# Attention in fewer, longer runs under the first dense layer, and lower halves of weights on VectorE during their conversion

## The chip, the cores and the metric

One core of one Trainium2 chip. The time is in device microseconds (us), the median of three runs: 896.46 before the change (895.49 to 898.31). All shares, spans and rows come from one profiled execution.

## The reference

Three stages follow each other. Sparse attention over 4 batches, 8 heads, 576 positions, 64 wide; half of the heads see the last 32 positions, the other half every 32nd. Its output, as 2304 tokens of 512, goes through a dense layer and then through a mixture of eight experts with a greedy assignment of tokens.

```python
scores = scale * np.matmul(q, k.transpose(0, 1, 3, 2))
attn = softmax(np.where(masks, scores, -1e9))          # local or strided mask by head
x = (attn @ v).transpose(0, 2, 1, 3).reshape(2304, 512)
h = x @ w_in                                           # 512 x 2048, float64 inputs
x = np.maximum(0.01 * h, h) @ w_out                    # 2048 x 512, float64 inputs
order = np.argsort(-(x @ w_gate).flatten())            # greedy: 8 experts, 288 tokens each
out[mask] = np.maximum(x[mask] @ w1[e], 0.0) @ w2[e]   # for each expert e
```

## The kernel before

**Attention** works on 16 units (a batch and two heads, one unit per 128 columns of the model width), each in two groups of two or three tiles. `attention()` is a pipeline of steps, one group entering per step: `a_tr` transposes queries and keys (L123), `a_qk` makes the scores of each tile for two heads (L167) and then masks, reduces (VectorE, L158) and exponentiates them (ScalarE, L160), `a_norm` divides on GpSimd (L182), `a_pt` transposes the probabilities (L195, with fillers L193 in the first five units), `a_pv` makes the value products (L210) and writes the tokens' upper and lower halves (L234, L235). In the program a float32 product of L167 or L210 is one instruction; the profile counts two for each.

**The dense layer** works in six blocks of 384 tokens and 16 slices n of 128 hidden columns each. Each 32-bit product is made of three: upper with upper, upper with lower, lower with upper half. `g1(n)` is 4 x 3 products into one PSUM bank (L374 to L376), the activation (L382 to L385) and then `g2(n)` adds 3 x 3 products to three banks of 512 columns, tag p2, kept for a whole block (L398 to L400, copied out at L405 and L407). Slice n = 16 begins block 1, and needs 16 finished attention groups (DONE); blocks 3 to 5 need 32.

**The weights** come as float64. `conversion()` makes 32 float32 tiles of 128 x 512 (a WI and a WO for each n of block 0): a load of 512 KB issued on GpSimd's queue into one of two buffers (L307, L310), ScalarE (L321), three VectorE instructions (L323 to L325), which free the buffer for the load after the next. `split()` then makes a tile's upper half on ScalarE (L350; or VectorE, L352) and its lower half on GpSimd (L353). CONV counts conversions.

**What sets the order.** Generators are advanced from the loop at the end: per piece of the dense layer a credit is added, and each whole credit advances attention by one piece, a `yield` of `attention()`. The first loop runs attention until DONE is 8. From this text a scheduler fixes each engine's own order of instructions: it takes in time what has its inputs and its buffer ready. PSUM buffers are shared by tag: units 0 to 4 take scores of their second group and the second transposed probabilities from the three banks of tag p2, which the dense layer's blocks use too.

From n = 48 on (second half of the dense layer and the experts) the text is the same before and after.

Of the kernel before, what the change touches and what calls it, by code (L numbers as in the profile page):

```python
# [7 lines left out]
F32 = mybir.dt.float32  # L8
# [18 lines left out]
def body(ctx, tc, q, k, v, w_in, w_out, w_gate, w1, w2, out):  # L27
    nc = tc.nc
# [51 lines left out]
    def xtile(j):  # L80
        if j not in XH:
            if j in (2, 3):
                XH[j], XL[j] = (xa.tile([128, 4, BLK], F32R, name="x" + x, tag=f"x{x}{j}") for x in "hl")
            else:
                XH[j], XL[j] = (xp.tile([128, 4, BLK], F32R, name="x" + x, tag="x" + x) for x in "hl")
        return XH[j], XL[j]
# [51 lines left out]
    def group(u, g):  # L138

        if u % 4 < 2:  # L140
            return 96, 128, [(96 * i, 96 * i, ml0 if i == 0 else ml, i) for i in range(3 * g, 3 * g + 3)]
        w = 18 * RG[2 * g][1]
        return w, w, [(18 * RG[i][0], 32 + 18 * RG[i][0], msf, i) for i in ((0, 1), (2, 3, 4))[g]]
# [3 lines left out]
    def a_qk(u, g):  # L147
        nq, nk, tl = group(u, g)
        n = len(tl)
        tag = "p2" if u < 5 and g else "pS"  # L150
        p = [ps.tile([128, 4, 128], F32, name=f"pS{h}", tag=tag, bufs=BUFS[tag]) for h in range(2)]
        s = at.tile([126, 2, 3, 128], F32, name="sc", tag="sc", bufs=3)
        mx = at.tile([126, 3, 2, 3], F32, name="mx", tag="mx", bufs=4)
        SC[u, g] = s, mx

        def score(i, m):
            for h in range(2):
                nc.vector.tensor_tensor_reduce(s[:nq, h, i, :nk], p[h][:nq, i, :nk], m[:nq, :nk], -0.125,  # L158
                                               3.0e38, OP.add, OP.min, mx[:nq, 0, h, i:i + 1])
                nc.scalar.activation(s[:nq, h, i, :nk], s[:nq, h, i, :nk], AF.Exp,  # L160
                                     bias=mx[:nq, 0, h, i:i + 1], scale=-1.0,
                                     accum_out=mx[:nq, 1, h, i:i + 1])

        for i, (q0, k0, m, _) in enumerate(tl):
            for h in range(2):
                r = slice(64 * h, 64 * h + 64)
                nc.tensor.matmul(p[h][:nq, i, :nk], QK[u][r, 0, 32 + q0:32 + q0 + nq],  # L167
                                 QK[u][r, 1, k0:k0 + nk], start=True, stop=True)
            if u < 2 and i:
                nc.tensor.matmul(p[0][:, 3], ident, QK[u][:, 0, 32:160], start=True, stop=True)  # L170
            yield
        for i, t in enumerate(tl):
            score(i, t[2])

# [26 lines left out]
    def a_pv(u, g):  # L201
        b, c = divmod(u, 4)
        nq, nk, tl = group(u, g)
        n = len(tl)
        t = PT.pop((u, g))
        tag = "p1" if u < 2 else "pT"
        p = ps.tile([128, 3 * 126], F32, name="pX", tag=tag, bufs=BUFS[tag])
        for i, tt in enumerate(tl):
            for h in range(2):
                nc.tensor.matmul(p[64 * h:64 * h + 64, i * nq:i * nq + nq], VT[u][:nk, tt[3], h, :],  # L210
                                 t[:nk, h, i, :nq], start=True, stop=True)
            if i == 0:
                yield
        pieces = []
        if c < 2:
            s0 = b * S + 288 * g
            o = 0
            while o < 288:
                j, a0 = divmod(s0 + o, BLK)
                w = min(288 - o, BLK - a0)  # L220
                pieces.append((p[:, o:o + w], *(x[:, c, a0:a0 + w] for x in xtile(j))))
                o += w
        else:
            r0, nr = 14 * g, n * nq // 18
            i0 = 0
            while i0 < 18:
                j, a0 = divmod(b * S + 32 * i0, BLK)
                i1 = min(18, i0 + (BLK - a0) // 32)
                pieces.append((p[:, :n * nq].rearrange("p (r i) -> p r i", i=18)[:, :, i0:i1],
                               *(x[:, c, a0:a0 + 32 * (i1 - i0)].rearrange("p (i r) -> p r i", r=32)[:, r0:r0 + nr]  # L230
                                 for x in xtile(j))))
                i0 = i1
        for src, dh, dl in pieces:
            (nc.scalar.copy if u else nc.vector.tensor_copy)(dh, src)  # L234
            nc.vector.tensor_sub(dl, src, dh.bitcast(F32))  # L235

    seq = [(u, g) for u in range(16) for g in range(2)]
    DONE = [0]

    def attention():  # L240

        for u in range(2):
            a_load(u)
        for u in range(2):
            v_load(u)
        for t in range(3):
            a_tr(0, t)
            yield
        n = len(seq)
        for s in range(n + 3):  # L250
            cur, mid, old = (seq[x] if 0 <= x < n else None for x in (s, s - 2, s - 3))
            u, g = cur or (99, 0)
            A = a_qk(u, g) if cur else iter(())
            V = a_pv(*old) if old else iter(())
            if u + 1 < 16 and s >= 1:
                a_tr(u + 1, g)
                yield
            if cur:
                next(A)
                yield  # L260
            if mid:
                a_pt(*mid, 0)
                yield
            if cur:
                next(A, None)
                yield
            if old:
                next(V)
                yield
            if u + 1 < 16 and g == 1:  # L270
                a_tr(u + 1, 2)
                yield
            if cur:
                next(A, None)
                yield
            if mid:
                a_pt(*mid, 1)
                yield
            for _ in A:
                pass  # L280
            if s < 1:
                a_tr(u + 1, g)
                yield
            if cur:
                a_norm(u, g)
            for _ in V:
                pass
            if old:
                DONE[0] += 1
            yield  # L290
            if g == 0 and u + 2 < 16:
                a_load(u + 2)
                v_load(u + 2)
# [49 lines left out]
    CONV = [0]  # L343

    def split(pool, src, tag, n):

        hi = pool.tile([128, 512], F32R, name="hi", tag=tag + "h", bufs=2)
        lo = pool.tile([128, 512], F32R, name="lo", tag=tag + "l", bufs=2)
        if n or EARLY[0]:
            nc.scalar.activation(hi, src, AF.Copy)  # L350
        else:
            nc.vector.tensor_copy(hi, src)  # L352
        nc.gpsimd.tensor_sub(lo, src, hi.bitcast(F32))  # L353
        return hi, lo


# [5 lines left out]
    def prep(n):  # L362

        if n < 96:
            SI[n] = split(xp, WI[n % 16], "wi", 0)
# [66 lines left out]
    def logits(pl, gs, f):  # L432

        if f % 4 == 2 and f > 3 or f == 15:
            c = f // 4 - (f < 15)
            for a in range(4):
                nc.tensor.matmul(pl[32 * a:32 * a + 32], V[:, 4 * c + a], gs[c][:, a], start=(c == 0), stop=(c == 3))

# [81 lines left out]
    for a in range(64, 128, 32):  # L520
        nc.vector.tensor_add(sel32, sel32, ident[:, a:a + 32])
    V = consts.tile([128, 16, 32], F32, name="V")
    nc.gpsimd.memset(V, 0.0)

    def gate_out():
        for f in range(0, 16, 3):
            fs = range(f, min(f + 3, 16))
            yield from gate([WO[x] for x in fs], V[:, f:f + len(fs), :8])

    A, Cv = attention(), conversion()  # L530
    bg = []
    for n, _ in enumerate(A):
        if n % 10 == 0:
            next(Cv, None)
        if DONE[0] >= 8:
            break
    credit = 0.0
    for n, _ in enumerate(mlp()):
        st = STEP[0]
        EARLY[0] = st < 20  # L540
        FIRST[0] = st >= 16
        if st < 16:
            if n == 0:
                next(Cv, None)
            credit += 0.9 if DONE[0] < 16 else 0
        elif st < 64:
            credit += 0.5 if DONE[0] < 32 else 0
        if n == 20:
            for a in range(4):
                nc.sync.dma_start(WB[32 * a:32 * a + 32, :, 8 * a:8 * a + 8], w_gate.rearrange("(b j) e -> j b e", j=32))  # L550
        if n == 98:
            bg.append(gate_out())
        if bg and n % 2 == 0:
            if next(bg[0], 1) == 1:
                bg.pop(0)
        while credit >= 1:
            next(A, None)
            credit -= 1
# [507 lines left out]
```

## Time and profile before

| what | value |
|---|---|
| median of three runs | 896.46 us (895.49 to 898.31) |
| the profiled execution's own time | 891.85 us |
| its span, first to last instruction | 890.1 us |
| TensorE busy, mean granted clock | 842.4 us (95%), 0.978 |
| VectorE, ScalarE, GpSimd busy | 544.8, 441.5, 492.1 us |

How to read it: a busy TensorE is not one at its peak, since each product's end is modelled and overlaps the next product's start; the distance from one start to the next tells what a product costs. Idle time of an engine off the critical path costs nothing. The profiled execution is 4.6 us under the median.

### The profile page before, as it was taken

To read this page: it belongs to the slowest core of one execution; us is meant where nothing else is said; L and a number is where in the kernel's file an instruction comes from. 1 tells how busy PE (TensorE), PEld (TensorE's weight loads), DVE (VectorE), ACT (ScalarE), POOL (GpSimd) and SP (SyncE) were. 2 spreads that over 40 slices of the span, in tenths; PEclk is the share of its full clock that TensorE was granted. 3 is DMA by queue.
4 is the path that set the end of the run, shared out by engine and by line. 5 is a ranking of instruction groups with operands and counts; after the bars stand their busy time and mean duration, and the time that the engine had idled before them with its cause. 6 is when DMAs were issued, how large, how long until landed. Compare 5 with 4: busy or idle time off the path is not lost. (4 is left out here: it accounts for less than half of the span.)

```text
span 890.1 us, 17029 instructions
## 1 busy us (share of the span) xinstructions
PE 842.4 (95%) x6272; PEld 710.9 (80%) x6272; DVE 544.8 (61%) x1552; ACT 441.5 (50%) x1098; POOL 492.1 (55%) x402
## 2 busy tenths in 40 slices
PE   8799999899999999999999999997999999999994
PEld 5677766677777787788989777775899999899994
DVE  5787888865546565475645546454758878772320
ACT  5787667464546455444555323332544444444641
POOL 2655646564555565544645355575648547558731
PEclk8999989999999999999999999999899999999998
DMA  8587554420122000044000004362546445546510
GB/s 193 145 199 175 143 137 137 129 63 14 29 46 79 17 6 10 1 160 160 1 1 1 19 1 166 109 205 92 166 147 192 147 133 182 173 146 206 181 52 27
DMA packets 95411, 93.18 MB, mean 105 GB/s; under 512 B 66144, under 2 KB 74336, under 8 KB 95328
## 3 DMA queue, kind: packets, MB, share of 16 engines
q1 hardware_dynamic: 87648, 65.88, 26.0%
q0 software_dynamic: 7680, 26.22, 9.6%
q8 instruction: 49, 0.80, 0.4%
q14 instruction: 34, 0.28, 0.1%
HBM read 76.35 MB, written 15.73 MB: 103 GB/s over the span
## 5 line engine op out<-in xcount | busy, mean ns | idle before, releaser
L353 POOL TENSOR_TENSOR lo<-WI,hi 128x512 fp32r<-128x512 f32 x96 | 127.5, 1328 | 98.9 <-DVE hi L352 58.2
L353 POOL TENSOR_TENSOR lo<-WO,hi 128x512 fp32r<-128x512 f32 x96 | 125.9, 1312 | 88.3 <-ACT hi L350 88.1
L859 POOL TENSOR_TENSOR wlo<-raw,whi 128x1024 fp32r<-128x1024 f32 x48 | 116.8, 2445 | 26.7 <-ACT whi L858 21.7
L350 ACT ACTIVATE hi<-WO 128x512 fp32r<-128x512 f32 x96 | 60.6, 631 | 101.3 <-PE q L961 49.2
L374 PE MATMUL p<-xh,hi 128*128 128x384 f32 x192 | 75.7, 395 | 5.3 <-DVE g L383 5.3
L916 PE MATMUL g<-hh,whi 128*128 128x288 f32 x256 | 78.8, 308 | 0.4 <-DVE exl L879 0.4
L893 PE MATMUL g<-exh,whi 128*128 128x288 f32 x256 | 78.6, 308 | 0.0
L894 PE MATMUL g<-exl,whi 128*128 128x288 f32 x256 | 76.8, 301 | 0.0
L917 PE MATMUL g<-hl,whi 128*128 128x288 f32 x256 | 76.2, 298 | 0.4 <-DVE hl L901 0.4
L895 PE MATMUL g<-exh,wlo 128*128 128x288 f32 x256 | 76.3, 298 | 0.0
L918 PE MATMUL g<-hh,wlo 128*128 128x288 f32 x256 | 75.7, 296 | 0.0
L160 ACT ACTIVATE sc<-sc,mx 96x128 f32<-96x128 f32 (+2 forms) x176 | 67.6, 388 | 15.0 <-DVE mx L158 15.0
L858 ACT ACTIVATE whi<-raw 128x1024 fp32r<-128x1024 f32 x64 | 67.3, 1053 | 2.9 <-DMA raw<-in_moe_w_dram 2.9
L376 PE MATMUL p<-xh,lo 128*128 128x384 f32 x192 | 66.3, 345 | 1.4 <-POOL lo L353 1.2
L421 PE MATMUL p<-xh,hi 128*128 128x384 f32 x192 | 66.4, 346 | 0.0
L375 PE MATMUL p<-xl,hi 128*128 128x384 f32 x192 | 65.8, 343 | 0.2 <-DVE xl L235 0.2
L423 PE MATMUL p<-xh,lo 128*128 128x384 f32 x192 | 64.7, 337 | 0.7 <-POOL lo L353 0.7
L398 PE MATMUL p<-hi,gh 128*128 128x512 f32 x144 | 64.3, 446 | 0.7 <-ACT gh L384 0.7
L422 PE MATMUL p<-xl,hi 128*128 128x384 f32 x192 | 64.4, 335 | 0.0
L182 POOL TENSOR_TENSOR sc<-sc,mx 96x384 f32<-96x384 f32 (+2 forms) x64 | 52.2, 832 | 21.4 <-DVE mx L180 15.2
L932 POOL DMA_INDIRECT out_dram<-o,idx x24 | 24.3, 1011 | 70.4 <-ACT o L908 58.4
L400 PE MATMUL p<-hi,gl 128*128 128x512 f32 x144 | 57.4, 398 | 0.0
(210 smaller groups left out, 2294.3 us busy)
## 6 DMA issues: line engine op xcount, KB each, us to landing
raw<-in_moe_w_dram SPq DMA_DIRECT2D x64, 512.0 KB
wraw<-in_moe_w_in_dram POOLq DMA_DIRECT2D x16, 512.0 KB
wraw<-in_moe_w_out_dram POOLq DMA_DIRECT2D x16, 512.0 KB
g<-g3d SPq DMA_DIRECT2D x16, 384.0 KB
rawq<-in_q_dram SPq DMA_DIRECT2D x32, 144.0 KB
rawk<-in_k_dram SPq DMA_DIRECT2D x32, 144.0 KB
x2d<-x SPq DMA_DIRECT2D x18, 256.0 KB
g3d<-gh SPq DMA_DIRECT2D x16, 192.0 KB
```

The costliest lines, as they stand in the source:

```text
L160: nc.scalar.activation(s[:nq, h, i, :nk], s[:nq, h, i, :nk], AF.Exp, bias=mx[:nq, 0, h, i:i + 1], scale=-1.0, accum_out=mx[:nq, 1, h, i:i ...
L353: nc.gpsimd.tensor_sub(lo, src, hi.bitcast(F32))
L374: nc.tensor.matmul(p1, wh[:, cs], xh[:, c], start=(c == 0), stop=False)
L421: nc.tensor.matmul(p1, wh[:, cs], xh[:, c], start=(c == 0), stop=False)
L858: pin(nc.scalar.activation(hi, raw, AF.Copy))
L859: pin((nc.vector if n in (5, 7) else nc.gpsimd).tensor_sub(lo, raw, hi.bitcast(F32)))
L893: nc.tensor.matmul(p, wh, xh[:, c], start=(c == 0), stop=False)
L894: nc.tensor.matmul(p, wh, xl[:, c], start=False, stop=False)
L895: nc.tensor.matmul(p, wl, xh[:, c], start=False, stop=(c == 3))
L916: nc.tensor.matmul(p, wh, hh[:, j], start=(j == 0), stop=False)
L917: nc.tensor.matmul(p, wh, hl[:, j], start=False, stop=False)
L918: nc.tensor.matmul(p, wl, hh[:, j], start=False, stop=(j == 7))
```

## The change

All scores of a group (two or three tiles, two heads) form one piece, and all its value products one. A step of attention then has five or six pieces in place of eight or nine, and the credits fall from 0.9 to 0.6 and from 0.5 to 0.33; conversions start every six pieces of the first loop, not ten. DONE is counted right behind the value products. Lower halves go to VectorE while CONV is at most 31, which is 31 of the 192 (16 of WI, 15 of WO).

```diff
@@ a_qk
             if u < 2 and i:
                 nc.tensor.matmul(p[0][:, 3], ident, QK[u][:, 0, 32:160], start=True, stop=True)
-            yield
+        yield
         for i, t in enumerate(tl):
             score(i, t[2])
@@ a_pv
                                  t[:nk, h, i, :nq], start=True, stop=True)
-            if i == 0:
-                yield
@@ attention
             if cur:
                 next(A, None)
-                yield
             if old:
-                next(V)
+                a_pv(*old)
+                DONE[0] += 1
                 yield
             if u + 1 < 16 and g == 1:
                 a_tr(u + 1, 2)
                 yield
-            if cur:
-                next(A, None)
-                yield
             if mid:
                 a_pt(*mid, 1)
                 yield
-            for _ in A:
-                pass
...
-            for _ in V:
-                pass
-            if old:
-                DONE[0] += 1
-            yield
@@ split
-        nc.gpsimd.tensor_sub(lo, src, hi.bitcast(F32))
+        (nc.gpsimd if CONV[0] > 31 else nc.vector).tensor_sub(lo, src, hi.bitcast(F32))
@@ the loops at the end
-        if n % 10 == 0:
+        if n % 6 == 0:
             next(Cv, None)
...
-            credit += 0.9 if DONE[0] < 16 else 0
+            credit += 0.6 if DONE[0] < 16 else 0
         elif st < 64:
-            credit += 0.5 if DONE[0] < 32 else 0
+            credit += 0.33 if DONE[0] < 32 else 0
```

In the changed file lines behind `a_pv` are lower: L374 to L376 become L361 to L363, L398 to L400 become L385 to L387, L323 to L325 become L310 to L312, L353 becomes L340, L383 and L385 become L370 and L372.

**The order, place one.** TensorE in block 1, before: scores (pS) of one tile between products of g2.

```order
L398 MATMUL p_2379<-hi,gh 128x512
L399 MATMUL p_2379<-lo,gh 128x512
L400 MATMUL p_2379<-hi,gl 128x512
L167 MATMUL pS_3072<-qk 108x108
L167 MATMUL pS_3073<-qk 108x108
L398 MATMUL p_2380<-hi,gh 128x512
L399 MATMUL p_2380<-lo,gh 128x512
L400 MATMUL p_2380<-hi,gl 128x512
```

The same group's scores with the change, the three tiles in one run:

```order
L385 MATMUL p_2377<-hi,gh 128x512
L386 MATMUL p_2377<-lo,gh 128x512
L387 MATMUL p_2377<-hi,gl 128x512
L167 MATMUL pS_3088<-qk 108x108
L167 MATMUL pS_3089<-qk 108x108
L167 MATMUL pS_3088<-qk 108x108
L167 MATMUL pS_3089<-qk 108x108
L167 MATMUL pS_3088<-qk 108x108
L167 MATMUL pS_3089<-qk 108x108
L385 MATMUL p_2378<-hi,gh 128x512
```

From the slice n = 17 to the end of attention the runs of attention between dense products are 109 before and 76 with the change; in these runs the change has 4 more transposes (L123) and 6 more of probabilities (L195), and as many scores and value products.

**Place two.** TensorE at the start of block 0, before. p_1056, p_1057 and p_1058 are the block's three banks of tag p2; the pP there is the last of units 0 to 4, of tag p2 too.

```order
L400 MATMUL p_1056<-hi,gl 128x512
L193 MATMUL pP<-ident 128x128 x3
L195 MATMUL pP<-ident,sc 128x96 x3
L398 MATMUL p_1057<-hi,gh 128x512
L399 MATMUL p_1057<-lo,gh 128x512
L400 MATMUL p_1057<-hi,gl 128x512
L210 MATMUL pX<-pt,vt 64x96 x3
L374 MATMUL p_1110<-xh,hi 128x384
L398 MATMUL p_1058<-hi,gh 128x512
```

The same pP with the change stands at the end of block 0 (p_1056 is its third bank, p_2234 the first slice of block 1):

```order
L385 MATMUL p_1056<-hi,gh 128x512
L386 MATMUL p_1056<-lo,gh 128x512
L193 MATMUL pP<-ident 128x128 x3
L195 MATMUL pP<-ident,sc 128x96 x3
L387 MATMUL p_1056<-hi,gl 128x512
L210 MATMUL pX<-pt,vt 64x96 x11
L123 MATMUL pT<-ident,rawq 128x96 x2
L123 MATMUL pT<-ident,rawk 128x96 x2
L361 MATMUL p_2234<-xh,hi 128x384
L195 MATMUL pP<-ident,sc 128x96 x3
```

Before, at the first product of slice n = 16, nine products of g2 of block 0 are still to come; with the change they stand ahead of this place. With the change no attention instruction stands on TensorE from the first quarter of the slice n = 4 to this place. Between it and the second slice of block 1 stand 34 scores, 37 value products, 29 transposes of probabilities and 32 transposes of queries and keys, and the last three quarters of the slice n = 16 among them; ScalarE has there 34 exponentials, 12 copies of pt, 12 of xh, 8 of qk and one upper half.

**Place three.** VectorE in the last conversions of block 0, before:

```order
L383 TENSOR_TENSOR g<-p_2086,g 128x384
L325 SCALAR_TENSOR_TENSOR WI<-wraw,cg 128x512
L385 TENSOR_TENSOR gl<-g,gh 128x384
L323 TENSOR_SCALAR cg<-cg 128x512
L324 SCALAR_TENSOR_TENSOR cg<-wraw,cg 128x512
L325 SCALAR_TENSOR_TENSOR WO<-wraw,cg 128x512
L323 TENSOR_SCALAR cg<-cg 128x512
```

And with the change:

```order
L312 SCALAR_TENSOR_TENSOR WI<-wraw,cg 128x512
L310 TENSOR_SCALAR cg<-cg 128x512
L311 SCALAR_TENSOR_TENSOR cg<-wraw,cg 128x512
L340 TENSOR_TENSOR lo<-WI,hi 128x512
L312 SCALAR_TENSOR_TENSOR WO<-wraw,cg 128x512
L340 TENSOR_TENSOR lo<-WO,hi 128x512
L310 TENSOR_SCALAR cg<-cg 128x512
L370 TENSOR_TENSOR g<-p_2126,g 128x384
L311 SCALAR_TENSOR_TENSOR cg<-wraw,cg 128x512
```

Two lower halves per pair of conversions stand among the conversion's own three instructions. GpSimd's order has, in this stretch, only loads and the divisions of attention.

## Rows read from the trace of the kernel before

**Rows 1.** Windows: length; busy PE, PEld, DVE, ACT, POOL; clock; DMA share, GB/s.
```profile
150.00:184.00 34.00, 28.53 (x179) 21.90 (x179) 29.07 (x55) 18.46 (x44) 19.62 (x19) 0.95 0.35 103
184.00:374.00 190.00, 190.00 (x1373) 149.69 (x1372) 103.81 (x341) 99.31 (x299) 104.39 (x93) 1.00 0.12 31
```

**Rows 2.** Timeline, TensorE: value products among dense ones; start, us, instruction, count.
```profile
243.27 0.55 PE L210 MATMUL pX<-pt,vt 128*64 128x96 f32 x8
243.75 0.50 PE L398 MATMUL p<-hi,gh 128*128 128x512 f32 x1
...
337.26 0.39 PE L400 MATMUL p<-hi,gl 128*128 128x512 f32 x1
337.58 0.39 PE L210 MATMUL pX<-pt,vt 128*64 128x96 f32 x4
337.89 0.50 PE L398 MATMUL p<-hi,gh 128*128 128x512 f32 x1
338.23 0.39 PE L399 MATMUL p<-lo,gh 128*128 128x512 f32 x1
338.46 0.39 PE L400 MATMUL p<-hi,gl 128*128 128x512 f32 x1
```

**Rows 3.** Groups of TensorE before 184.2 us; then the timeline behind it.
```profile
L374 PE MATMUL p<-xh,hi 128*128 128x384 f32 x64 | 26.9, 420 | 5.3 <-DVE g L383 5.3
```
```profile
184.32 0.44 PE L374 MATMUL p<-xh,hi 128*128 128x384 f32 x1
```

**Rows 4.** Timeline, VectorE: block 0's first activation; the twelfth conversion's last instruction.
```profile
71.96 0.56 DVE L383 TENSOR_TENSOR g<-p,g 128x384 f32<-128x384 f32 x1
...
80.84 1.48 DVE L325 SCALAR_TENSOR_TENSOR WO<-wraw,cg 128x512 int32<-128x512 int32 x1
```

**Rows 5.** Timeline: a lower half on GpSimd, and VectorE beside it.
```profile
127.35 1.75 POOL L353 TENSOR_TENSOR lo<-WO,hi 128x512 fp32r<-128x512 f32 x1 [1.60 <-ACT hi L350]
```
```profile
127.88 1.50 DVE L323 TENSOR_SCALAR cg<-cg 128x512 int32<-128x512 int32 x1
```

**Rows 6.** Timeline: two loads into one buffer, and conversions on VectorE about them.
```profile
163.06 0.81 POOL L307 DMA_DIRECT2D wraw<-in_moe_w_in_dram  x1 [2.83 <-DVE WI L325]
...
170.61 0.79 POOL L307 DMA_DIRECT2D wraw<-in_moe_w_in_dram  x1 [2.70 <-DVE gl L385]
```
```profile
164.31 1.42 DVE L325 SCALAR_TENSOR_TENSOR WO<-wraw,cg 128x512 int32<-128x512 int32 x1
...
169.36 0.68 DVE L325 SCALAR_TENSOR_TENSOR WI<-wraw,cg 128x512 int32<-128x512 int32 x1
...
177.12 0.65 DVE L325 SCALAR_TENSOR_TENSOR WI<-wraw,cg 128x512 int32<-128x512 int32 x1
```

**Rows 7.** Two lines' VectorE subtractions: least, median, longest ns; starts; shape.
```profile
L859 DVE TENSOR_TENSOR wlo<-raw,whi x16: 1215/1223/3835, 631.3 to 858.4; 128x1024 fp32r<-128x1024 f32 x16
```
```profile
L385 DVE TENSOR_TENSOR gl<-g,gh x48: 508/558/1645, 73.4 to 373.3; 128x384 fp32r<-128x384 f32 x48
```

**Rows 8.** Groups of ScalarE: count, busy us, mean ns, idle before, releaser.
```profile
L160 ACT ACTIVATE sc<-sc,mx 96x128 f32<-96x128 f32 (+2 forms) x176 | 67.6, 388 | 15.0 <-DVE mx L158 15.0
...
L350 ACT ACTIVATE hi<-WI 128x512 fp32r<-128x512 f32 x37 | 23.2, 628 | 10.7 <-PE p L422 5.0 <-PE p L375 2.5 <-DVE WI L325 1.7
...
L197 ACT ACTIVATE pt<-pP 128x288 f32<-128x288 f32 (+2 forms) x51 | 20.3, 404 | 8.2 <-PE pP L195 8.0
L134 ACT ACTIVATE qk<-pT 128x384 f32<-128x384 f32 (+1 forms) x48 | 20.2, 429 | 21.2 <-PE pT L123 10.8 <-DVE qk L136 9.8
L234 ACT CAST xh<-pX 128x168 fp32r<-128x168 f32 (+6 forms) x53 | 19.8, 373 | 7.7 <-DVE xl L235 3.9 <-PE pX L210 3.8
```

**Rows 9.** Windows, line L160 alone (exponentials and their sums' readouts, half each).
```profile
48.00:73.00 25.00, 10.68 (x50) 1.00 0.79 195
```

**Rows 10.** Timeline, TensorE at 1.2 GHz: window 100 to 125 us.
```profile
116.81 0.44 PE L374 MATMUL p<-xh,hi 128*128 128x384 f32 x1 [1.66 <-DVE g L383]
...
123.28 0.63 PE L399 MATMUL p<-lo,gh 128*128 128x512 f32 x1
```

More of the change, by code (lines that the diff above doesn't have):

```diff
@@ L253, in attention @@
             A = a_qk(u, g) if cur else iter(())
-            V = a_pv(*old) if old else iter(())
             if u + 1 < 16 and s >= 1:
```

## The prediction

> **What bounds the kernel now.** I read the windows first, then TensorE's timeline, then the two other engines' timelines around the conversions. From 184 to 374 us, blocks 1 and 2 of the dense layer with attention's second half, TensorE is busy throughout at its full clock, while VectorE and ScalarE are busy for little over half of the time [rows 1]: there a microsecond of TensorE is a microsecond of the whole. Before that it is another matter. In block 0 it is idle for 5.5 of the 34 us from 150 to 184 [rows 1]; GpSimd's load sits there until a conversion has freed its buffer [rows 6], and the block ends when the last weights are converted. So the part up to the slice n = 16, which begins at 184.3 us with 64 first products (16 slices of 4) behind it [rows 3], is priced by conversions, and the part behind it by TensorE.
>
> **The runs of attention behind n = 16.** Four value products between dense ones make 0.97 us from the start of the dense product ahead to that of the second one behind (337.26 to 338.23); two dense starts alone would be 2 x 0.23 (338.23 to 338.46) [rows 2]. So such a run costs 0.51. Eight in one run take 0.48 to the next dense start, where four take 0.31 [rows 2]: four more cost 0.17. A run joined to another saves 0.34. For scores no row has a long run in this stretch; their saving lies between nothing and the whole 0.51, and I take the value products' 0.34, which have the same two instructions per product. The order has 33 runs fewer there (76 for 109): 33 x 0.34 = 11.2 us. The 4 + 6 transposes that the change has more, at a quarter of 0.31 each, give back 0.8. Net **-10.4 us**; bounds 0 (if something else becomes the limit) and -16. Block 0's own joined runs I cost at nothing: the conversions hide them, and without that cover each would be worth another 0.34.
>
> **The conversions.** A lower half on GpSimd holds VectorE up: L323 took 1.50 us and ended 0.28 after the lower half beside it had ended [rows 5]; L325 took 1.42 in one place and 0.68 in another [rows 6]. With the change no lower half is on GpSimd before the conversions end. In their place VectorE gets 31. It has no row for 512 columns: the same subtraction took 0.56 at 384 and 1.22 at 1024 columns (medians), which are the bounds, and the line through them gives 0.69 [rows 7]. GpSimd's queue has then loads and divisions alone, so no load is issued later than before.
>
> When attention is over, a buffer goes round in 7.55 us (163.06 to 170.61) [rows 6]: that is two conversions, one in each buffer. In that round one instruction of VectorE was held up by 0.74 (1.42 less 0.68) [rows 6]. Without it: 6.8. The new order puts one lower half into a buffer's chain between two of its instructions and one beside it: I add 0.69 once, **7.5 us a pair**. The bounds are 6.8 (both in gaps) and 9.45 (both in the chain, each with its upper half of 0.63 [rows 8] waited for: 6.8 + 2 x 1.32).
>
> The start: the twelfth conversion ended at 82.3 [rows 4]. With the change it stands right behind block 0's first activations, whose first was at 72.0 [rows 4]; attention sets that, and I leave it. Behind it come some 3 us of activation, scores and conversion; I take 76. The thirty-first, the last that block 0's TensorE work needs early, is 9.5 pairs on: 76 + 9.5 x 7.5 = 147.3. Before, it ended at 177.8 [rows 6], and n = 16 began 6.5 us later [rows 3] with nine products of g2, 2.1 us at 0.23, still ahead. So the block's end is at 147.3 + 8.6 = **155.9 us**.
>
> **What takes their place.** The early end is not a gain yet. All three p2 banks are now taken by block 0 before the last pP of that tag is ready, and it can be written only when the block has left; everything of attention behind it waits too. Thus attention for block 1, hidden before beside slow conversions, stands by itself between the blocks. ScalarE's work there is 34 exponentials, 12 pt, 12 xh, 8 qk and an upper half: 34 x 0.388 + 12 x 0.404 + 12 x 0.373 + 8 x 0.429 + 0.63 = 26.6 us [rows 8], the lower bound. The upper one is the pace of 48 to 73 us, where attention ran nearly alone, with four conversions: 25 exponentials in 25 us [rows 9], so 34 us. I take the middle, 30. It ends at **185.9 us**, with slice n = 16 and block 0's second layer done. Before, that state came at 184.3 + 2.1 for the nine products and 2.1 for the slice (twelve products of 384 columns, 0.23 x 384 / 512 each): 188.5. The first 16 slices and attention for block 1 thus change by **-2.6 us**: the conversions' gain is spent on attention that has lost its cover.
>
> From n = 48 on the work is the same, so nothing. The sum is -10.4 - 2.6 = -13.0. The profiled execution's own time of 891.85 becomes 878.9; it stands 4.6 us under the median, and 896.5 - 13.0 gives a median of **883.5 us**.
>
> **The rivals.**
>
> *VectorE holds the conversions back.* Its queue is in order: a lower half whose upper half ScalarE has not yet made stops the next conversion behind it, and the loads that wait for its buffer. At the upper bound of 9.45 us a pair, 9.5 x 1.95 = 18.5 us come on top: 902.0, slower. For it speaks the order, where the lower half of WO stands right behind its conversion; against it, that VectorE waited for ScalarE's conversions with time to spare in the round above, and that half of the lower halves have an activation or a conversion ahead of them. It decides from 8.9 us a pair on, where the whole gain is gone.
>
> *TensorE's clock falls between the blocks.* With attention alone TensorE has gaps. After an idle stretch of 1.66 us at 115 us it ran at 1.2 GHz: L399 took 0.63 where it takes 0.39 at 2.4 GHz [rows 10, 2]. Some 70 products at the 0.08 of rows 2 for each of their two instructions, and 61 transposes at as much, are 16 us at full clock. At half clock 16 more, of which ScalarE's 26.6 us hide what they don't wait for; I take 6, between 0 and 16: 889.5. Against it, in the conversions' gaps from 150 to 184 us the clock was still 0.95 [rows 1]. The Trainium skill, page "TensorE: Matmul & The Clock Gate", section "What's actually happening", speaks for it: the throttled clock is the default, and only activity releases it. By that rule the 6 us belong in the sum; by the row they don't, and I left them out.
>
> *The joined runs are worth nothing.* If the single bank of g1 or VectorE's bursts of scores become the limit behind n = 16, the 10.4 us stay: 893.9. Against it stand VectorE's 104 busy of 190 us and a TensorE without idle time there [rows 1].
>
> *The loads alone set the pace.* Lower halves in the gaps at 6.8 a pair, and ScalarE at its floor: -6.7 - 3.4, so 873.4.
>
> **How the numbers follow.** Chances: forecast 0.42, VectorE 0.23, clock 0.13, loads alone 0.12, joined runs worthless 0.10. About 0.3%, 2.7 us, is what a measurement tells from no change. Forecast, clock and loads alone are faster by more (0.67), the worthless runs lie within it (0.10), VectorE's case is slower (0.23). The range is 873 to 902: from loads alone to VectorE's full price. What it leaves out is a sum of misfortunes (the longest attention stretch upon the slowest pace) and joined runs at more than I gave. The forecast's own range, from 7.0 to 8.0 us a pair and 28 to 32 us between the blocks, is 877 to 890.
>
> **What would show it.** Right: the thirty-first conversion near 147 us; no instruction of VectorE beside a lower half stretched before it; lower halves there near 0.69; then some 30 us with exponentials close together on ScalarE, TensorE with gaps and hardly a dense product; n = 17 begun near 186 us; from there to the end of block 2 some 10 us less with TensorE still without gaps; the rest as before. Wrong: conversions that end near 165 us with VectorE's lower halves waiting for ScalarE; a stretch between the blocks far from 30 us; TensorE at 1.2 GHz in it; or blocks 1 and 2 as long as before.

## The result, and the profile after

The changed kernel takes **906.66 us** (904.93 to 913.66, five runs), where the one before took 896.46 in the same runs: the ratio is 1.0113, 95% interval 1.0087 to 1.0139. It is slower; 883.5 was forecast and 902 was the end of the range.

The profiled execution of the changed kernel is its longest, 7 us above its median, and that of the kernel before lies 4.6 under its own. So both were profiled once more, at 908.04 and 897.94. These two are near their medians, and the stages in the table are theirs. A stage runs from one mark to the next, all read from the timelines: the first product of a slice, and ScalarE's copy of block 0's second result bank.

| stage, us | before | after | change | forecast |
|---|---|---|---|---|
| start, to n = 1 | 78.0 | 82.1 | +4.1 | 0 |
| n = 1 to block 0's copy | 115.7 | 92.4 | -23.3 | -30.5 |
| copy to n = 17 | 1.3 | 39.1 | +37.8 | +27.9 |
| n = 17 to n = 48 | 184.7 | 176.8 | -7.8 | -10.4 |
| n = 48 to the end | 516.3 | 515.8 | -0.6 | 0 |
| span | 896.1 | 906.2 | +10.1 | -13.0 |

Entries are rounded singly, so a sum can be off by 0.1. The forecast's entries are its own terms: block 0 ends at 155.9 for 186.4, and the stretch with slice 16 is 30 for 2.1. The stages that were to change went the way that was forecast, but each gained less or lost more, and the start lost too.

The windows of the first profile after, which answer to [rows 1] (length; busy PE, PEld, DVE, ACT, POOL; granted clock; DMA share, GB/s):

```profile
84.00:130.00 46.00, 42.82 (x230) 35.37 (x229) 39.41 (x80) 27.56 (x61) 10.34 (x15) 1.00 0.49 138
130.00:166.00 36.00, 26.63 (x110) 21.49 (x109) 26.86 (x48) 16.22 (x30) 5.73 (x9) 0.91 0.41 132
...
176.00:215.00 39.00, 32.42 (x249) 23.25 (x252) 15.23 (x97) 26.89 (x104) 10.84 (x15) 0.72 0.36 84
215.00:392.00 177.00, 177.00 (x1383) 147.74 (x1376) 104.34 (x346) 98.35 (x294) 99.35 (x90) 0.99 0.13 33
```

From 215 us on TensorE is without a gap again, as before. The loss stands ahead of that: 26.63 of 36 us busy in the last conversions, and 39 us between the blocks at a clock of 0.72.

VectorE's timeline after, at the marks of [rows 4] (block 0's first activation, the twelfth conversion's last instruction), then the last instructions of the 16th, the 20th and, as in [rows 6], the 31st and the 32nd conversion:

```profile
81.30 0.55 DVE L370 TENSOR_TENSOR g<-p,g 128x384 f32<-128x384 f32 x1
...
83.51 0.68 DVE L312 SCALAR_TENSOR_TENSOR WO<-wraw,cg 128x512 int32<-128x512 int32 x1
...
104.23 0.68 DVE L312 SCALAR_TENSOR_TENSOR WO<-wraw,cg 128x512 int32<-128x512 int32 x1
...
121.30 0.69 DVE L312 SCALAR_TENSOR_TENSOR WO<-wraw,cg 128x512 int32<-128x512 int32 x1
...
165.00 0.69 DVE L312 SCALAR_TENSOR_TENSOR WI<-wraw,cg 128x512 int32<-128x512 int32 x1
...
167.52 1.78 DVE L312 SCALAR_TENSOR_TENSOR WO<-wraw,cg 128x512 int32<-128x512 int32 x1
```

The twelfth ends 2.9 us behind the first activation, as forecast, but both come 8 to 9 us late; the 31st ends at 165.7, not at 147.3. Between them lie 9.5 pairs in 81.5 us, 8.58 a pair. That is a mean of different stretches. The first two pairs (84.2 to 104.9), beside the last of attention, take 10.4 us each; TensorE, busy for 19.78 us from 84.2 to 105.0, hardly waits there. The next two take 8.5 each, the 5.5 behind them 7.95. What fills a slow round, one round of a load buffer from the middle stretch shows: GpSimd's two loads into it, ScalarE's conversion and what VectorE does about it.

```profile
105.46 0.76 POOL L297 DMA_DIRECT2D wraw<-in_moe_w_out_dram  x1 [2.24 <-DMA wraw<-in_moe_w_in_dram]
...
114.64 0.54 POOL L297 DMA_DIRECT2D wraw<-in_moe_w_out_dram  x1 [3.68 <-DMA wraw<-in_moe_w_in_dram]
```
```profile
109.54 0.66 ACT L308 ACTIVATE cg<-wraw 128x512 f32<-128x512 f32 x1 [1.85 <-DMA wraw<-in_moe_w_out_dram]
```
```profile
110.23 0.43 DVE L310 TENSOR_SCALAR cg<-cg 128x512 int32<-128x512 int32 x1 [0.70 <-ACT cg L308]
110.62 0.56 DVE L370 TENSOR_TENSOR g<-p,g 128x384 f32<-128x384 f32 x1
111.13 0.69 DVE L340 TENSOR_TENSOR lo<-WI,hi 128x512 fp32r<-128x512 f32 x1
111.74 0.68 DVE L311 SCALAR_TENSOR_TENSOR cg<-wraw,cg 128x512 int32<-128x512 int32 x1
112.34 0.55 DVE L372 TENSOR_TENSOR gl<-g,gh 128x384 fp32r<-128x384 f32 x1
112.81 0.68 DVE L340 TENSOR_TENSOR lo<-WO,hi 128x512 fp32r<-128x512 f32 x1
113.42 0.69 DVE L312 SCALAR_TENSOR_TENSOR WO<-wraw,cg 128x512 int32<-128x512 int32 x1
```

The load takes 4.08 us from issue to ScalarE's start, ScalarE 0.66, VectorE 3.88 from 110.23 to 114.11, and the next load follows 0.53 later: 9.2 us. VectorE's own part for the conversion is 1.8; two lower halves and two activations stand between its three instructions. The engine waits for the load at the round's start and holds up the next load at its end: a bracket on GpSimd's rows can name a landing, but from the 14th conversion on every load is issued 0.54 to 0.56 us behind the VectorE instruction that frees its buffer. Later rounds have fewer such guests and take 6.9 to 8.7 us (122.53 to 130.48: 7.95).

TensorE between the blocks, the middle of the 39 us (last bracket: idle time before, and what ended it):

```profile
189.07 0.90 PE L167 MATMUL pS<-qk 64*96 64x128 f32 x12
190.76 0.46 PE L195 MATMUL pP<-ident,sc 108*108 108x108 f32 x3 [0.79 <-ACT qk L134]
194.03 0.55 PE L123 MATMUL pT<-ident,rawq 96*128 96x96 f32 x2 [2.80 <-issue]
194.37 0.63 PE L195 MATMUL pP<-ident,sc 126*126 126x126 f32 x2
194.93 1.17 PE L167 MATMUL pS<-qk 64*96 64x128 f32 x6
...
216.99 0.60 PE L363 MATMUL p<-xh,lo 128*128 128x384 f32 x1
217.43 0.34 PE L361 MATMUL p<-xh,hi 128*128 128x384 f32 x1
217.60 0.34 PE L362 MATMUL p<-xl,hi 128*128 128x384 f32 x1
```

Six records of scores take 1.17 us at 194.93, twelve took 0.90 at 189.07: after 2.80 idle us, for which the trace names no wait, TensorE is at 1.2 GHz. It then works almost without a gap, and the 2.4 GHz return only near 217. The repeat shows the same stretch, with 2.67 idle us and 1.2 GHz from 192 to 216.

The transposes that end the idle stretch read the queries of a unit's two heads. SyncE issued one head's load well before the other's, with loads of values between:

```profile
186.82 0.40 SPq L98 DMA_DIRECT2D rawq<-in_q_dram  x1
...
190.90 0.52 SPq L98 DMA_DIRECT2D rawq<-in_q_dram  x1
```

They begin 3.13 us behind the second issue; in the repeat it is 3.06 (189.24 to 192.30), in the run with lower halves on GpSimd below 3.25 (196.15 to 199.40). So the wait was probably for this load; since no landing is recorded, that is not shown.

### The profile page after: what moved, and what is told of

The parts are those of the page before. It is cut to its first block, busy times and chain, and to the rows that moved or that the text cites. A ratio compares the mean times of both kernels' runs of the same rounds, so it can differ in the third digit from the quotient of the medians.

```text
span 911.9 us, 17053 instructions
## 1 busy us (share of the span) xinstructions
PE 844.8 (93%) x6272; PEld 727.2 (80%) x6272; DVE 547.8 (60%) x1584; ACT 446.7 (49%) x1097; POOL 447.7 (49%) x371
## 5 line engine op out<-in xcount | busy, mean ns | idle before, releaser
L340 POOL TENSOR_TENSOR lo<-WI,hi 128x512 fp32r<-128x512 f32 x80 | 105.7, 1322 | 95.7 <-DVE hi L339 58.2
L340 POOL TENSOR_TENSOR lo<-WO,hi 128x512 fp32r<-128x512 f32 x81 | 104.3, 1289 | 86.4 <-ACT hi L337 86.3
L361 PE MATMUL p<-xh,hi 128*128 128x384 f32 x192 | 72.7, 379 | 9.4 <-DVE g L370 4.5
L160 ACT ACTIVATE sc<-sc,mx 96x128 f32<-96x128 f32 (+2 forms) x176 | 67.6, 386 | 19.4 <-DVE mx L158 19.1
L182 POOL TENSOR_TENSOR sc<-sc,mx 96x384 f32<-96x384 f32 (+2 forms) x64 | 50.3, 804 | 39.9 <-DVE mx L180 35.1
L363 PE MATMUL p<-xh,lo 128*128 128x384 f32 x192 | 66.5, 346 | 0.5 <-DVE lo L340 0.3
L385 PE MATMUL p<-hi,gh 128*128 128x512 f32 x144 | 61.1, 426 | 6.2 <-ACT gh L371 6.2
L408 PE MATMUL p<-xh,hi 128*128 128x384 f32 x192 | 66.2, 345 | 0.0
L387 PE MATMUL p<-hi,gl 128*128 128x512 f32 x144 | 57.8, 403 | 0.5 <-DVE gl L372 0.4
```

The lines of the kernel that those rows point to most:

```text
L340: (nc.gpsimd if CONV[0] > 31 else nc.vector).tensor_sub(lo, src, hi.bitcast(F32))
L361: nc.tensor.matmul(p1, wh[:, cs], xh[:, c], start=(c == 0), stop=False)
L363: nc.tensor.matmul(p1, wl[:, cs], xh[:, c], start=False, stop=(c == 3))
```

## The experiments

The theories: **B**, the early end of block 0 makes the last pP of tag p2 wait for the block's banks and lays attention for block 1 bare, which costs more than the conversions give; **V**, the prediction's rival, lower halves on VectorE hold the conversions back and are the loss. Later ones are named where they come up.

**Lower halves back on GpSimd.** Edit, on the changed kernel:

```diff
-        (nc.gpsimd if CONV[0] > 31 else nc.vector).tensor_sub(lo, src, hi.bitcast(F32))
+        nc.gpsimd.tensor_sub(lo, src, hi.bitcast(F32))
```

> The change with all lower halves back on GpSimd; the last pP of tag p2 still waits for block 0, so attention for block 1 still stands alone between the blocks. Theory B (the banks: attention that lost its cover costs the time): still slower than before, 900 to 912 us, the stretch between the blocks again 36 to 40 us. Theory V (lower halves on VectorE slow the start and the conversions): most of the 10 us come back, 885 to 895, with n = 1 near 73 us in place of 82 and the last conversion near 155 us.

912.63 us (908.26 to 914.51), ratio to before 1.0151 [1.0096, 1.0205]. V falls: without its suspect the kernel is no faster. From the twelfth to the 31st conversion it takes 88.1 us for 81.5; the stretch between the blocks is still there, with 35.4 us. Its VectorE shows what the change removed:

```profile
134.68 3.24 DVE L311 SCALAR_TENSOR_TENSOR cg<-wraw,cg 128x512 int32<-128x512 int32 x1
```
```profile
134.84 1.29 POOL L340 TENSOR_TENSOR lo<-WI,hi 128x512 fp32r<-128x512 f32 x1
136.09 1.28 POOL L340 TENSOR_TENSOR lo<-WO,hi 128x512 fp32r<-128x512 f32 x1
```

An instruction of 0.68 lasts 3.24 us here, beside two lower halves on GpSimd. The Trainium skill, page "SBUF — State Buffer", section "SBUF: two separate sides", says that VectorE with two inputs from SBUF and GpSimd share a port pair and that one blocks the other for a whole instruction. These rows agree in that the instruction ends 0.55 us behind the second lower half; which of them had the ports first they don't show (VectorE's is recorded as the first to start, by 0.16 us).

**Another bank for the last pP of tag p2.** Edit, on the changed kernel, in `a_pt`:

```diff
-        tag = "p2" if u < 5 and h else "pT"
+        tag = "p2" if (u < 4 or u == 4 and g == 0) and h else "pT"
```

> The change, but the last pP of tag p2 (unit 4, second group, second head) takes tag pT: nothing of attention waits for block 0's banks, and attention for block 1 stands among block 0's products again; lower halves stay on VectorE. Theory B: the stretch between the blocks is gone and attention is covered by conversions; blocks 1 and 2 keep their 8 us: 880 to 891 us. Theory V: conversions with attention and lower halves both on VectorE are slower still, so what the stretch gives back is lost in block 0: 896 to 910.

**880.33 us** (876.88 to 884.3), ratio 0.9816 [0.976, 0.9871]: 26 us from one bank, and faster than both kernels. n = 17 begins 0.3 us behind block 0's copy, for 39. The windows of its block 0 (columns as above):

```profile
100.00:125.00 25.00, 24.01 (x168) 19.59 (x167) 22.11 (x63) 19.68 (x62) 8.05 (x11) 1.00 0.64 161
125.00:150.00 25.00, 23.54 (x156) 19.07 (x155) 22.90 (x74) 19.21 (x66) 7.19 (x10) 0.93 0.55 146
150.00:182.00 32.00, 27.09 (x196) 21.07 (x195) 27.42 (x60) 15.89 (x33) 9.12 (x11) 0.95 0.36 107
```

Attention is back beside the conversions; these last longer for it (95.0 us from the twelfth to the 31st, for 81.5), and nothing is left to do between the blocks.

**Both edits together**: joined runs and lower rates alone, without bank wait or lower halves on VectorE.

> Joined runs and lower rates alone: the pP on tag pT and all lower halves on GpSimd. Theory B: block 0 as before (n = 16 near 184 us), blocks 1 and 2 shorter by 8 us: 885 to 891. Theory V: the same or better than the kernel with lower halves on VectorE and the pP on tag pT. If joined runs cost something in block 0 itself (longer bursts of TensorE there): above 893.

892.63 (890.2 to 900.19), ratio 0.9951 [0.992, 0.9981]: 1.6 over the range that B expects, and slower than the kernel above by 12: with the other bank, lower halves on VectorE are a gain. Slice n = 16 begins at 196.9 us, not near 184; n = 1 came at 85.3, while block 0 took 115.5, as before.

**Lower halves on VectorE in the kernel before**, and nothing else.

> The kernel before with only the lower halves on VectorE while converting; attention keeps its pieces and its place among block 0's products. Theory V: VectorE has 31 more instructions of 0.69 us where it bounds block 0, less what held it up: 899 to 910 us, conversions end later than 181 us. Theory B: lower halves on VectorE are about even with what they free: 891 to 898.

894.13 (890.58 to 899.43), ratio 0.9951 [0.9926, 0.9977], as B expects; from the twelfth to the 31st conversion 90.6 us for 95.5. Here too they are a gain, of 4 us by the medians.

**Products on the identity between the blocks.** Theory C: TensorE's clock makes the 39 us. Theory A: the chain through ScalarE does. Edit, on the changed kernel, in `a_pt`:

```diff
-        for _ in range(3 if u < 5 else 0):
+        for _ in range(3 if u < 9 else 0):
```

> The change, with three more products on the identity (as units 0 to 4 have them) ahead of each transpose group of probabilities for units 5 to 8 too: 36 of them stand in the stretch between block 0 and slice n = 17, for 3 in the change. Theory C (TensorE's clock): the change's trace has an idle 2.80 us on TensorE near 191 us and 1.2 GHz from there to 214 us, with TensorE then without gaps; products that fill the gap keep 2.4 GHz, and the stretch from the last copy of block 0 to n = 17 falls from 38.3 to about 32 us, the time from 906.7 to about 901. Theory A (the chain through ScalarE sets the stretch whatever the clock): the stretch stays at 36 to 40 us and the time at 906 to 909.

904.81 (903.99 to 907.06), ratio 1.0084 [1.0057, 1.011]; from copy to n = 17 it takes 36.0 us. The same stretch, first in the change and then here:

```profile
185.00:195.00 10.00, 5.68 (x55) 3.97 (x55) 4.26 (x35) 7.90 (x36) 2.72 (x5) 0.92 0.59 125
195.00:205.00 10.00, 9.92 (x62) 7.65 (x62) 3.42 (x20) 6.59 (x26) 1.61 (x2) 0.50 0.41 91
205.00:214.00 9.00, 8.69 (x45) 5.42 (x47) 3.17 (x18) 5.09 (x19) 3.23 (x4) 0.50 0.19 43
```
```profile
185.00:195.00 10.00, 9.32 (x84) 7.48 (x84) 4.57 (x32) 7.75 (x33) 2.71 (x5) 1.00 0.72 151
195.00:205.00 10.00, 9.84 (x92) 7.91 (x90) 5.04 (x33) 8.41 (x36) 3.22 (x4) 1.00 0.52 115
205.00:211.00 6.00, 5.94 (x81) 4.44 (x80) 3.91 (x12) 4.19 (x14) 2.85 (x3) 1.00 0.11 25
```

The clock stays at 2.4 GHz throughout, and the stretch is 3 us shorter, net of the 33 added products; the time lies between what the two theories expect, and its interval overlaps the change's. C explains a part. How large a part this run can't tell, since the added products take time themselves; the third load buffer below tells more. ScalarE is busy for 20.4 of these 26 us even so: a chain through it remains.

**Units 0 to 3 as before the change**, on the kernel with the other bank: pieces of a tile and a conversion each ten pieces until DONE is 8, joined runs behind (theory S: the order delays the start; N: the start varies).

> The change with the last pP in the banks of pT (as the run that took 880.3), and units 0 to 3 as before the change: scores and value products in pieces of a tile, conversions each ten pieces of the first loop. Joined runs only behind them. Theory S (the joined runs and the earlier conversions delay the start): n = 1 begins near 73 to 75 us for 77.4, and the time is 876 to 878. Theory N (the start differs from execution to execution, the order has no part in it): n = 1 between 73 and 83 us, the time 879 to 882.

883.46 (880.29 to 884.52), ratio 0.9831 [0.9803, 0.9858], n = 1 at 81.8. S expected 876 to 878, and no run came under 880.29: S falls, though by n = 1 alone, which is of one profile, it could not be told. The time is 1.5 over what N expects; by the intervals it is not to be told from 880.33.

**The two kernels once more**, word for word, for their profiles.

> The kernel before, word for word, for a second profile. Theory S: the start is set by the order, so n = 1 begins within 1.5 us of the first profile's 72.9. Theory N: the start differs from execution to execution; n = 1 is 3 us or more away from 72.9, towards the 80.7 that the kernel before with lower halves on VectorE showed. From n = 17 to n = 48 both expect 184.7, within 1 us, and behind it 515.8, within 3.

> The changed kernel, word for word, for a second profile; the first was 7 us above its median. Theory S: n = 1 within 1.5 us of 82.4. Theory N: 3 us or more earlier. Both expect 176.9 within 1 us from n = 17 to n = 48, and a stretch between block 0's last copy and n = 17 of 35 to 39 us with the clock at 1.2 GHz in its second half.

897.94 and 908.04. n = 1 begins at 78.0 and 82.1: before, the first profile's start was an early one, by 5 us, as N has it; after, it came out the same, as S has it. So neither theory holds for both. From n = 17 to n = 48 each kernel repeats itself to 0.1 us (184.7 twice, 176.9 and 176.8).

**A third load buffer**, in the place of the last two WI tiles, on the changed kernel. Theory L: a buffer's round sets the conversions' pace. Theory Q: VectorE's queue does.

```diff
...
-        raw = xa.tile([128, 1024], I32, name="wraw", tag=("xh3", "xl3")[n % 2])
+        raw = xa.tile([128, 1024], I32, name="wraw", tag=("xh3", "xl3", "WI7")[n % 3 if n < 27 else (n + 1) % 2])
...
-        if n + 2 < 32:
+        if n < 26:
+            w_load(n + 3)
+        elif n > 26 and n + 2 < 32:
             w_load(n + 2)
...
```

> The change with a third buffer for the loads of weights (the place of the last two WI tiles, which is free until the 29th conversion). In the change's trace a buffer goes round in 7.4 to 8.3 us from the 18th conversion on, of which the load takes 4.1 and the two loads' landing leaves ScalarE and VectorE waiting. Theory L (the round of a load buffer sets the pace): from the twelfth to the 31st conversion 60 to 70 us for 81.4, block 0's last copy at 155 to 165 us for 175, and as the stretch behind it stays, the time falls by 10 to 18 us, to 889 to 897. Theory Q (VectorE's queue, with its lower halves and activations between a conversion's instructions, sets the pace): 78 to 82 us, the time 903 to 908.

**888.71** (886.55 to 890.93), ratio 0.9883 [0.9849, 0.9916]: 18 us faster than the change, as L has it. But the 18 us were won partly in other places than it said:

```profile
100.00:125.00 25.00, 22.89 (x111) 18.89 (x110) 22.65 (x43) 15.83 (x30) 5.61 (x10) 1.00 0.48 148
125.00:147.00 22.00, 20.38 (x101) 17.50 (x100) 19.78 (x37) 12.00 (x23) 2.69 (x5) 1.00 0.40 120
159.00:192.00 33.00, 26.44 (x253) 19.23 (x252) 15.45 (x97) 26.55 (x105) 11.47 (x16) 0.89 0.41 98
```
```profile
146.42 0.69 DVE L315 SCALAR_TENSOR_TENSOR WI<-wraw,cg 128x512 int32<-128x512 int32 x1
```

The twelfth conversion ends at 70.6, 13 to 14 us earlier, beside attention at the start; behind it 76.6 us follow to the 31st, not 60 to 70. VectorE is now busy for 90% of the time and TensorE for 92%; which of them holds the pace there is not shown. So the two buffers bound the pace, and other limits stand close behind them. The 31st ends at 147.1 us and block 0's copy begins at 158.9.

The stretch between the blocks, which was to stay, is 33.3 us for 39.1. It holds the same work (the last window, beside the one from 176 to 215 in the change). The two loads of queries stand one behind the other here (169.36), the long idle stretch is missing, and TensorE is at a granted 1.00 to 180 us and at 0.50 only from 185 on. So the idle stretch and the fallen clock go with some 6 of the 39 us.

**The third buffer and the other bank.**

> The same third buffer in the change with the last pP in the banks of pT (880.3). There TensorE is idle for 8.8 of the 123 us from 77 to 200 us. Theory L: conversions end some 5 to 15 us earlier, but block 0 has its attention to do as well and TensorE little idle time left: 872 to 877. Theory Q: 879 to 882.

**874.68** (872.12 to 877.68), ratio 0.9725 [0.9693, 0.9757], inside what L expects: the best of all, 2.7% faster than before.

**Scores in pieces of a tile again** from unit 4 on, on the kernel with the other bank; value products stay joined.

```diff
...
-        yield
+            if DONE[0] >= 8:
+                yield
+        if DONE[0] < 8:
+            yield
...
             if cur:
                 next(A, None)
+                if DONE[0] >= 8:
+                    yield
...
+            if cur and DONE[0] >= 8:
+                next(A, None)
+                yield
...
-            credit += 0.6 if DONE[0] < 16 else 0
+            credit += 0.82 if DONE[0] < 16 else 0
...
-            credit += 0.33 if DONE[0] < 32 else 0
+            credit += 0.45 if DONE[0] < 32 else 0
```

> The change with the last pP in the banks of pT, but with scores in pieces of one tile again from unit 4 on (value products stay in one run; credits 0.82 and 0.45): 98 runs of attention behind n = 17, where that kernel has 73 and the one before the change 109. If a joined run of scores is worth as much as one of value products (184.7 less 173.2 over 36 runs is 0.32 us): 25 x 0.32 = 8.0 us more, 181 from n = 17 to n = 48 and 888. If joined scores are worth nothing: 173 to 175 and 880 to 882.

890.37 (887.05 to 897.31), ratio 0.991 [0.9882, 0.9937]; 183.5 us from n = 17 to n = 48, for 173.2. Its TensorE, and that of the kernel with joined scores:

```profile
268.37 0.34 PE L373 MATMUL p<-xh,lo 128*128 128x384 f32 x1
268.64 0.46 PE L167 MATMUL pS<-qk 64*96 64x128 f32 x4
269.03 0.44 PE L371 MATMUL p<-xh,hi 128*128 128x384 f32 x1
269.31 0.34 PE L372 MATMUL p<-xl,hi 128*128 128x384 f32 x1
```
```profile
268.09 0.34 PE L363 MATMUL p<-xh,lo 128*128 128x384 f32 x1
268.36 0.90 PE L167 MATMUL pS<-qk 64*96 64x128 f32 x12
269.19 0.45 PE L361 MATMUL p<-xh,hi 128*128 128x384 f32 x1
269.47 0.34 PE L362 MATMUL p<-xl,hi 128*128 128x384 f32 x1
```

A tile alone takes 0.94 us between the first dense start and the third, three tiles 1.38. Dense starts lie 0.17 apart (217.43 to 217.60 in the change), so 0.34 of each is dense: 0.60 three times against 1.04, 0.38 saved per join. The stage agrees. From n = 17 to n = 48 the timelines have 94 runs here and 70 with joined scores (the expectation counts to the end of attention, which lies behind n = 48), and it takes 10.3 us more. Some of that is work: 140 records of scores and 79 of transposed probabilities, for 128 and 76. At 0.055 a record of scores (1.04 for 12, 0.60 for 4) and 0.08 a transpose that is about 0.9 us, an estimate, and 0.39 a run are left. The kernel before has 9 runs more (103), with 128 and 73 records, and takes 184.7 - 183.5 = 1.2 us longer in spite of 1.1 us less such work. So the runs of value products are worth some 0.25 each, by difference alone.

**Fewer conversions at the start**, a conversion each nine pieces of the first loop, on the best kernel.

> The kernel that took 874.7 (banks and third load buffer), with a conversion each nine pieces of the first loop in place of six: four fewer while units 0 to 3 stand alone. If conversions at the start hold attention up (in that kernel n = 1 began at 84.4 us and the twelfth conversion ended at 69.6, 14 us ahead of its use): n = 1 at 77 to 80 and 869 to 873. If not, the conversions come later for nothing: n = 1 within 2 us of 84.4 and 875 to 880.

877.49 (872.8 to 879.3), ratio 0.9753 [0.9711, 0.9794], n = 1 at 83.5, as expected where conversions don't hold the start up.

## Why the prediction was wrong

It forecast 883.5 and a gain; the kernel is slower by 1.1%. The mechanisms it names are all there. What failed are the sizes of its terms, all to one side. The first two below are one stage, the stretch between the blocks.

**"I take the middle, 30."** The attention that lost its cover takes 39.1 us from copy to n = 17, 9.9 us more than the term allowed. ScalarE's work was right: 26.6 us forecast, 26.89 busy in the window of 39 us. The middle assumed that ScalarE would be kept busy for nine tenths. Without the idle stretch, and with the clock up for most of the time, the run with a third buffer still needed 33.3. The upper bound, 34, which came from a place where attention did run nearly alone, was the row of the same kind and should have been taken: the middle is wrong by about 4 of the 9.9.

**The clock rival, at 0.13, came true on top of that.** TensorE fell to 1.2 GHz and stayed there from 194 to 217 us. With the idle stretch ahead of it this makes the other 6 of the 9.9 us (39.1 for 33.3), and 6 were named; what the clock alone costs no run separates (with added products, 3 came back net). The argument against it, a clock of 0.95 from 150 to 184 [rows 1], was of a stretch with dense products. The Trainium skill's rule that only activity releases the clock, in "TensorE: Matmul & The Clock Gate", section "What's actually happening", pointed the right way; but here 18.6 busy us of 19 (195 to 214) did not release it, which the rule as told there doesn't lead one to expect.

**"7.5 us a pair."** It was 8.58. The 7.55 of [rows 6] is a real round, but one from where attention is over, with one activation instruction (168.90) among the conversion's own three. I added one lower half to it and used it from the twelfth conversion on, where attention still ran for two pairs. Of the 10.3 us too much, 7.8 lie in the first four pairs, at 10.4 and 8.5 a pair; in the round above two lower halves and two activations stand between the conversion's instructions. The 5.5 pairs behind them, at 7.95, are within the forecast's own 7.0 to 8.0. That a third buffer brings the 31st conversion to 147.1 (forecast 147.3) is luck: there the twelfth ended 5 us ahead of the forecast's 76, and the pace was 8.06. The rival that named VectorE as the brake had part of the pace right (8.58 lies between 7.5 and its 9.45), but lower halves on VectorE are not the loss: by medians they are a gain of 4 us in the kernel before (898.55 in those runs), 6 in the change (3 by the ratios, whose intervals overlap) and 12 with the other bank.

**"The start: attention sets that, and I leave it."** n = 1 came 9 to 10 us later than in the profile that I read, of which 5 are that profile's early start and 4 the change. The last 4 are not explained: going back on joined runs and on more conversions at the start did not bring n = 1 forward (81.8, 83.5, one profile each), and the kernel before with lower halves on VectorE had n = 1 at 80.7, while lower halves on GpSimd in the change had it at 83.1.

**"A run joined to another saves 0.34."** As a mean it was near: 33 runs fewer from n = 17 to n = 48 (70 for 103) saved 11.5 us with the other bank, 0.35 each. But scores are worth about 0.4, and value products, from whose rows the 0.34 was read, some 0.25 by difference. The "four value products" of that row are records of the profile, two products of the program. The change itself kept 7.8 of the 10.4. Its stage begins with 2 us at 1.2 GHz, and it holds work that the kernel with the other bank has done by then: 32 and 16 more of the small gating products (L468, L474), ten more transposes and three more runs. What each of these costs was not measured.

**What was right:** the bank that the pP waits for, the attention laid bare behind it, TensorE without gaps behind n = 17, and nothing from n = 48 on. The working had block 0 30.5 us shorter and the stretch 27.9 longer, a difference of two large terms that left -2.6. The gain came out 24% smaller, the loss 35% larger, and the difference at +14.4. The range, ending at 902, had room for the misses of the stretch and of the conversions (9.9 and 7.2), not for those of the start and the runs as well.

## What to carry to other kernels

Work that one stage hides in another is free only while the stage that hides it stays long. Before a stage is shortened, look for what is written into its banks or buffers and must now wait for its end, and move that first: here one PSUM tag was worth 26 us, and with it the change is a gain of 1.8%.

Where a forecast is a small difference of two large terms, its uncertainty is that of the terms, and a price for work that will run alone is best taken from a row where it did run alone.

A buffer's round is load, conversion, every instruction that the order puts between, and issue; when it sets the pace, another buffer may help (here one in a tile not yet written, 18 us).

## What the runs showed that was not expected

TensorE stayed at 1.2 GHz for some 24 us (193.5 to 217.4) while it was busy for 18.6 of the 19 us from 195 to 214, with attention's products of 96 to 128 columns, its transposes and a few dense products; with 33 products more ahead of the same transposes it never fell. The 2.80 us of idle time before the fall end 3.13 us behind the issue of a load that stood behind others in SyncE's queue.

An unchanged kernel's start differs by 5 us between two executions (n = 1 at 72.9 and 78.0), while its later stages repeat to 0.1 us (184.7) and 0.5 (515.8, 516.3): a term taken from the start should be read from more than one profile. The start's length goes with TensorE's mean granted clock up to n = 1: 0.93 and 0.89 in the two executions of the kernel before, 0.85 in both of the change (82.4 and 82.1). That is not all of it, since with the other bank it was 0.93 and n = 1 came at 77.4; and which of the two causes the other no run shows.
